# Early keys of pass 2 in larger loads, values' products ahead of scores, and w_in and w_out blocks in pairs, in a two-layer decode kernel on one core

## The chip, the core and the metric

The kernel runs on one core of a Trainium2 chip. Its engines are TensorE (PE, with its weight loads as PEld), VectorE (DVE), ScalarE (ACT), GpSimd (POOL) and SyncE (SP), which here only issues DMAs. Each engine works through its own instructions in the order in which they were written and stops where a semaphore tells it to wait. The metric is the device time of one execution, in microseconds. The kernel before takes 1320.69 us (median of 3 runs, 1320.47 to 1320.93).

## What is computed

Two transformer layers of a decode step, and both layers use the same weights and the same cache. Batch is 2, the model's width 448; there are 16 heads of width 256, a cache of 4096 keys and values for each head and sequence, and a gated feed-forward part of width 1792. All data are float32.

```python
def _A_ref(x, k_cache, v_cache, wq, wo):
    q = (x @ wq).reshape(B, Sq, H, Dh).transpose(0, 2, 1, 3)
    scores = jnp.einsum("bhqd,bhkd->bhqk", q, k_cache) * (Dh ** -0.5)
    p = _softmax(scores, axis=-1)
    o = jnp.einsum("bhqk,bhkd->bhqd", p, v_cache)
    return o.transpose(0, 2, 1, 3).reshape(B, Sq, H * Dh) @ wo

def _B_ref(x, W_gate, W_up, W_down):
    gate = jnp.einsum("bsd,df->bsf", x, W_gate)
    up = jnp.einsum("bsd,df->bsf", x, W_up)
    gate = gate * (gate > 0)
    return jnp.einsum("bsf,fd->bsd", gate * up, W_down)

x = A_x
x = x + _A_ref(_layernorm(x), A_k_cache, A_v_cache, A_wq, A_wo)
x = x + _B_ref(_layernorm(x), B_W_gate, B_W_up, B_W_down)
x = x + _A_ref(_layernorm(x), A_k_cache, A_v_cache, A_wq, A_wo)
x = x + _B_ref(_layernorm(x), B_W_gate, B_W_up, B_W_down)
```

The cache is far larger than the core's memory and is read twice, once for each layer, apart from a few blocks that stay in place between the layers.

## The kernel before, in words

**Pairs and units.** A pair `u` is one head of one sequence; there are 32, numbered 0 to 31 in each pass (a pass is one layer). The keys of a pair are a block of 128 partitions x 8192 numbers, and so are its values. A block has four pieces, `c` = 0 to 3, of 128x2048 numbers, 1 MiB each. One tile, `arena`, holds everything that is read from memory: 27 units of one piece each. Weights come into the same units: `w_head` for each head (query and output weights), and for the feed-forward part seven blocks of `w_in` and four of `w_out`, each 128x1792 or less.

**Loads.** `pending` is a list of loads in a fixed order. `pump` (L116 to L138) takes the first one, asks `units` for as many neighbouring free units as it needs, and writes its DMA on SP's queue (L131). A load of 1 piece is `128x2048`, one of 4 pieces `128x8192`, one of 8 pieces (the keys of a pair together with the values of the pair before it) `128x16384`. A load of 4 or 8 pieces needs 4 or 8 units that stand side by side. `release` frees a unit behind the last instruction that reads it and calls `pump` again. All this is decided when the program is written; on the chip SP waits at each DMA for the readers of the units that it overwrites. So a load waits for its own units and for every load ahead of it in the list.

**Scores and values.** For a pair in the middle, DVE multiplies the whole key block with the query (L378, one instruction of 128x8192) and sums (L386); for some pairs, 5 to 8 of pass 2 among them, 8 of the 32 sums are left to ACT (L382). In the first pairs of pass 2 the pieces are taken one by one: DVE multiplies half a piece in one instruction (L409), ACT sums that half (L411), and DVE multiplies and sums the other half in four instructions (L418). `softmax_max` is L427 on DVE and L429 on POOL, `softmax_exp` L434 and L437 on ACT and L443 on POOL. `weigh` (L462) multiplies the probabilities with the values on PE: 16 matmuls for a pair, four for each piece. Its result stands in `po`, in one half for even and the other for odd pairs. `out_copy` (L475, ACT) and `out_add` (L478, DVE) take it out, `out_turn` (L488, PE), `out_keep` (L501, DVE) and `project` (L511, PE) bring it to the output, and `query` (L338 and L342 on PE, L350 on ACT, L354 on POOL) makes the next head's queries. An instruction of a matmul shows as two records in the profile, so 16 matmuls of L462 are x32.

**The order around the change.** The loop at L527 writes one step for each `u`: scores of `u`, values of `u - 1`, output of `u - 2`. In the first five steps of pass 2 (`mixed`, `u` below `HASTE` = 5) the four pieces of `weigh(u - 1)` are spread between the four pieces of scores; in later steps they come at the end. Pass 2 begins with 20 units kept from pass 1 and its pairs run in another order (`second`). `WHOLE_SECOND` tells which pairs of pass 2 have their keys in loads of 8 pieces; `early` and `at_end` cut others into smaller loads.

Of the kernel before, what the change touches and what calls it, by code (L numbers as in the profile page):

```python
# [14 lines left out]
B, D, H, S, DH, F = 2, 448, 16, 4096, 256, 1792  # L15
P = 128
# [4 lines left out]
UNIT = CT * DH  # L21
NC = NT // CT
BLOCKS, SINGLES = 3, 3
PAIR = 2 * NC
WHOLE_FIRST = range(1, 28)
WHOLE_SECOND = range(9, 29)
KEPT = 20
ALONE = 25

# [41 lines left out]
def two_layers(  # L71
# [20 lines left out]
    arena = consts.tile([P, (BLOCKS * PAIR + SINGLES) * UNIT], F32, name="arena")  # L92
# [4 lines left out]
    units = Arena()  # L97
    pending = []
    at_of = {}
    blocks = set()  # L100

    def source(key, n):
        kind, name, c = key
        if kind in "kv":
            h, b = name
            at = (h * B + b + (kind == "v")) % (H * B)
            c += NC * (kind == "k" and n < PAIR)
            return vk[at, :, c * UNIT : (c + n) * UNIT]
        if kind == "h":
            return w_head[name]  # L110
        if kind == "in":
            return w_in[c]
        return w_out[:, 14 * P * c : min(14 * P * (c + 1), 14 * D)]

    def pump():
        while pending:  # L116
            (kind, name, c), n = pending[0]
            last = at_of.get((kind, name, c - 1)) if kind in "kv" else None
            at = units.take(n, kind, last)
            if at is None:  # L120
                return
            pending.pop(0)
            src = source((kind, name, c), n)
            dst = arena[:, at * UNIT : at * UNIT + src.shape[1]]
            parts = [0, src.shape[1]]
            if not pending:
                parts[1:1] = [src.shape[1] - CLOSE * TAIL]
            elif len(pending) == 1:
                parts[1:1] = [8 * P]
            for i, j in zip(parts, parts[1:]):  # L130
                nc.sync.dma_start(dst[:, i:j], src[:, i:j])  # L131
            for k in range(n):
                key = (kind, name, c + k)
                if n == PAIR:
                    key = ("k", name, k - NC) if k >= NC else ("v", behind[name], k)
                at_of[key] = at + k
            if n >= NC:
                blocks.add((kind, name))  # L138

    def get(*key):  # L140
        at = at_of[key]
        return arena[:, at * UNIT : (at + 1) * UNIT]

    def release(*key):
        units.free.add(at_of.pop(key))
        pump()

    first = [(h, b) for h in range(H) for b in range(B)]
# [3 lines left out]
    def loads(order, whole, cuts):  # L152


        found = [(("h", order[0][0], 0), 1)]

        def some(kind, u):
            c = 0
            for n in cuts.get((kind, u), (NC,)):
                found.append(((kind, order[u], c), n))  # L160
                c += n

        for u, unit in enumerate(order):
# [11 lines left out]
    ffn_loads = [("in", "", c) for c in range(7)] + [("out", "", c) for c in range(4)]  # L175
    n_u = len(first)
    each = (1,) * NC
    twos = (2,) * (NC // 2)
    final = (2, 1, 1)
    at_end = {("k", n_u - 1): twos, ("v", n_u - 2): twos, ("v", n_u - 1): final}  # L180
    of_first = loads(first, WHOLE_FIRST, at_end)
    at_end[("k", n_u - 2)] = twos
    early = {(kind, u): each for u in range(HASTE + 1) for kind in ("kv" if u < HASTE else "k")}
    of_second = loads(second, WHOLE_SECOND, early | at_end)

    keep = {of_second[0][0], *[key for key, _ in of_second if key[0] != "h"][:KEPT]}
    keep.add(("v", second[2], NC - 1))
    of_second = [(key, n) for key, n in of_second if key not in keep]

    heads = [(key, n) for key, n in of_second if key[0] == "h"][:2]  # L190
    of_second = [part for part in of_second if part not in heads]
    of_second[NC - 1 : NC - 1] = heads
    pending += of_first + [(key, 1) for key in ffn_loads]
    pending += of_second + [(key, 1) for key in ffn_loads]

    row = consts.tile([P, 2 * DH], F32, name="row")
    down = consts.tile([P, D], F32, name="down")
# [94 lines left out]
    def inverse():  # L292
        nc.vector.reciprocal(rstd, rstd)

    def attention(order, after, q_first=None, begun=None):
# [6 lines left out]
        n_u = len(order)  # L302
# [67 lines left out]
        def score_block(u, c):  # L370
# [6 lines left out]
            if c == 0:  # L377
                nc.vector.tensor_mul(kt, kt, q_of[u][:, None, :].to_broadcast([P, NT, DH]))  # L378
            shared = 0 if (WHOLE_SECOND if ahead else WHOLE_FIRST)[0] <= u < ALONE else CT
            if c == 0:  # L380
# [10 lines left out]
        def score(u, c):  # L391
# [30 lines left out]
            if not kept:  # L422
                release("k", order[u], c)
# [96 lines left out]
        def if_pair(step, u, *more):  # L520
            if 0 <= u < n_u:
                step(u, *more)
# [4 lines left out]
        for u in range(n_u + 2):  # L527

            mixed = ahead and u < HASTE
            if_pair(score, u, 0)  # L530
            if_pair(out_add, u - 2)
            if_pair(out_turn, u - 2)
            if mixed:
                if_pair(weigh, u - 1, 0)
            if_pair(score, u, 1)
            if mixed:
                if_pair(weigh, u - 1, 1)
            if_pair(score, u, 2)
# [246 lines left out]
def _arrays(np, A_x, A_k_cache, A_v_cache, A_wq, A_wo, B_W_gate, B_W_up, B_W_down, **_):  # L785

    def pairs(cache):
        return cache.transpose(1, 0, 2, 3).reshape(H * B, P, NT * DH)

    rows = FULL * P  # L790
    wq = A_wq.reshape(D, H, DH)
    head = [wq[c * P : (c + 1) * P].transpose(1, 0, 2) for c in range(FULL)]
    head.append(wq[rows:].reshape(TAIL, H, 2, P).transpose(1, 2, 0, 3).reshape(H, P, P))
    wo = A_wo.reshape(H, 2, P, D)
    head += [wo[:, 0], wo[:, 1]]
    full = [w[c * P : (c + 1) * P] for w in (B_W_gate, B_W_up) for c in range(FULL)]
# [4 lines left out]
    found = {  # L801
        "x": A_x,
        "vk": np.concatenate([np.roll(pairs(A_v_cache), 1, 0), pairs(A_k_cache)], axis=2),
        "w_head": np.concatenate(head, axis=2),
        "w_in": np.stack(full),
        "w_out": np.concatenate(
            [c[:, at : at + P] for at in range(0, D, P) for c in chunks], axis=1
        ),
    }
    return {n: np.ascontiguousarray(a) for n, a in found.items()}  # L810


def build(nc, shapes):
    import concourse.tile as _tile

    args = [
        nc.dram_tensor(f"in_{n}_dram", s, F32, kind="ExternalInput").ap() for n, s in shapes.items()
    ]
    for i, (shape, _) in enumerate(_OUTS):
        args.append(nc.dram_tensor(f"out_{i}_dram", shape, F32, kind="ExternalOutput").ap())  # L820
    with _tile.TileContext(nc) as tc:
        two_layers(tc, *args)
# [12 lines left out]
```

## Time and profile before

| | |
|---|---|
| runs of the kernel before | 1320.47, 1320.69, 1320.93 us |
| the profiled execution | 1320.27 us |
| its span, first to last instruction | 1318.5 us |
| read from memory | 562.56 MB, 427 GB/s over the span |
| busy: DVE / PE / POOL / ACT | 1081.6 / 553.7 / 269.0 / 195.6 us |
| DMA queue of SP | 22612 packets, 99.5% of 16 engines' span |

In a row of the timeline the first number is the start in us from the beginning of the span, the second the time it took; then come engine, line, operation, what is written and read, the shape, and in brackets how long the engine had been idle and what ended that. In a row of stages (`A:B`) each engine's busy time is followed by PE's granted clock as a share of full speed, the share of the time in which the 16 DMA engines were busy, and the rate in GB/s. Pass 2 begins near 690 us.

### The profile page before, as it was taken

The page shows a single profiled execution, that of the slowest core. Times are in us where ns is not written, and L with a number is a line of the kernel's source. Part 1 is how long each engine was busy: PE and PEld are TensorE (multiplying, and loading weights), DVE is VectorE, ACT ScalarE, POOL GpSimd, SP SyncE. Part 2 cuts the span into 40 slices and gives each one's busy share as a digit, 9 for nine tenths or more (in the row PEclk, how much of TensorE's full clock was granted, in tenths as well). Part 3 has the DMA queues.
Part 4 walks back from the last instruction along what each step waited for, and adds up shares of the span by engine and source line. Part 5 has one row for each costly group of instructions (what it writes and reads, how often), then busy time and mean ns, then how long its engine had stood idle before and what let it go on. Part 6 is the DMA issues. An engine that isn't in the chain of part 4 may idle for free.

```text
span 1318.5 us, 9085 instructions
## 1 busy us (share of the span) xinstructions
PE 553.7 (42%) x3276; PEld 190.6 (14%) x3276; DVE 1081.6 (82%) x780; ACT 195.6 (15%) x776; POOL 269.0 (20%) x192
## 2 busy tenths in 40 slices
PE   2243342433434324345585444242433424434348
PEld 2011010110111101112141111110111101101113
DVE  4989888898888988888729987798888988877892
ACT  2100000000000000212026513000000000012241
POOL 0002003322133220321001153030123331230210
PEclk9675666656667667666697777666767667666679
DMA  9999999999999999999999999999999999999998
GB/s 408 435 430 429 432 428 437 432 436 434 417 445 435 430 430 426 445 418 430 421 405 416 431 430 435 438 432 430 432 431 436 433 428 436 429 432 425 427 425 334
DMA packets 22665, 563.16 MB, mean 427 GB/s; under 512 B 2520, under 2 KB 2652, under 8 KB 9564
## 3 DMA queue, kind: packets, MB, share of 16 engines
q1 hardware_dynamic: 22612, 562.57, 99.5%
q8 instruction: 26, 0.43, 0.1%
q14 instruction: 19, 0.16, 0.0%
q10 hardware_dynamic: 8, 0.00, 0.0%
HBM read 562.56 MB, written 0.00 MB: 427 GB/s over the span
## 4 chain that ended last, share of the span: by engine, by line
DMA 55%; DVE 32%; PE 7%; POOL 2%; issue 2%; ACT 1%; DVEq 0%; SPq 0%; POOLq 0%; ACTq 0%
DMA arena<-in_vk_dram 54%; DVE arena L378 12%; DVE scores L386 11%; DVE arena L409 3%; DVE down L418 2%; PE po L462 2%; POOL top L429 2%; DVE arena L418 2%; DMA arena<-in_w_out_dram 1%; DVE row L478 1%; PE small L488 1%; PE acc L511 1%; DVE scores L415 1%; ACT arena L411 1%; PE pf L576 1%
## 5 line engine op out<-in xcount | busy, mean ns | idle before, releaser
L378 DVE TENSOR_TENSOR arena<-arena 128x8192 f32<-128x8192 f32 x51 | 443.3, 8692 | 111.0 <-DMA arena<-in_vk_dram 110.9
L386 DVE TENSOR_REDUCE scores<-arena 128x32 f32<-128x8192 f32 (+1 forms) x53 | 431.8, 8148 | 0.0
L488 PE MATMUL small<-ones,row 128*128 128x1 f32 x256 | 62.0, 346 | 686.3 <-DVE row L478 686.3
L462 PE MATMUL po<-arena,probs 128*2 128x512 f32 x2048 | 303.1, 734 | 10.3 <-DMA arena<-in_vk_dram 6.6
L429 POOL PARTITION_ALL_REDUCE top<-mx x64 | 64.6, 1009 | 645.8 <-DVE mx L427 645.8
L443 POOL PARTITION_ALL_REDUCE total<-rs x64 | 176.1, 2752 | 61.3 <-ACT probs L437 60.3
L488 PEld LDWEIGHTS small<-ones,row 128*128 128x128 f32 x256 | 56.5, 308 | 748.9 <-DVE row L478 748.9
L434 ACT ACTIVATE nm<-top,nsr 128x1 f32<-128x1 f32 x64 | 18.8, 294 | 612.4 <-POOL top L429 612.4
L354 POOL PARTITION_BROADCAST arena<-arena x58 | 27.6, 545 | 300.6 <-ACT arena L350 300.6
L462 PEld LDWEIGHTS po<-arena,probs 128*2 128x2 f32 x2048 | 54.8, 96 | 198.3 <-issue 191.2
L338 PE MATMUL pq<-arena,xs 128*33 128x256 f32 x174 | 70.6, 571 | 14.1 <-DMA arena<-in_w_head_dram 14.1
L511 PE MATMUL acc<-arena,oT 128*2 128x448 f32 x128 | 50.9, 894 | 32.1 <-DVE oT L501 32.1
L350 ACT ACTIVATE arena<-pq 33x256 f32<-33x256 f32 x29 | 10.9, 377 | 321.7 <-PE pq L342 321.7
L382 ACT ACTIVATE arena<-arena 128x256 f32<-128x256 f32 x104 | 41.7, 402 | 86.2 <-DVE arena L378 86.2
L478 DVE SCALAR_TENSOR_TENSOR row<-po,lead,row 128x256 f32<-128x256 f32 x64 | 30.7, 479 | 25.8 <-ACT row L475 25.4
L411 ACT ACTIVATE arena<-arena 128x256 f32<-128x256 f32 x117 | 47.1, 404 | 20.4 <-DVE arena L409 20.1
L409 DVE TENSOR_TENSOR arena<-arena 128x1024 f32<-128x1024 f32 (+1 forms) x24 | 42.0, 1748 | 0.0
L338 PEld LDWEIGHTS pq<-arena,xs 128*33 128x33 f32 x174 | 25.3, 162 | 81.3 <-issue 66.7
L475 ACT ACTIVATE row<-po,lead 128x256 f32<-128x256 f32 x64 | 29.1, 455 | 21.2 <-PE po L462 21.2
L418 DVE SCALAR_TENSOR_TENSOR down<-arena,pq 128x256 f32<-128x256 f32 x64 | 26.9, 420 | 5.4 <-DMA arena<-in_vk_dram 3.4
L501 DVE TENSOR_TENSOR oT<-small,ri 128x4 f32<-128x4 f32 x32 | 5.1, 161 | 29.0 <-PE small L488 29.0
L437 ACT ACTIVATE probs<-scores,nm,sr 128x32 f32<-128x32 f32 x64 | 26.4, 413 | 2.1
(145 smaller groups left out, 359.0 us busy)
## 6 DMA issues: line engine op xcount, KB each, us to landing
arena<-in_vk_dram SPq DMA_DIRECT2D x16, 4096.0 KB, 40.0
arena<-in_w_head_dram SPq DMA_DIRECT2D x31, 896.0 KB, 30.9
arena<-in_vk_dram SPq DMA_DIRECT2D x27, 1024.0 KB, 14.9
arena<-in_vk_dram SPq DMA_DIRECT2D x12, 2048.0 KB, 38.5
arena<-in_w_in_dram SPq DMA_DIRECT2D x14, 896.0 KB, 26.2
arena<-in_w_out_dram SPq DMA_DIRECT2D x5, 896.0 KB, 8.9
arena<-in_vk_dram SPq DMA_DIRECT2D x47, 43.4
arena<-in_w_out_dram SPq DMA_DIRECT2D x1, 512.0 KB, 17.3
```

The source lines that it names most:

```text
L338: nc.tensor.matmul(q, xs[:, c, :], w[:, c * DH : (c + 1) * DH], start=(c == 0), stop=False)
L378: nc.vector.tensor_mul(kt, kt, q_of[u][:, None, :].to_broadcast([P, NT, DH]))
L386: nc.vector.reduce_sum(s_of[u][:, shared:], kt[:, shared:, :], axis=AX.X)
L409: nc.vector.tensor_mul(some, some, q_of[u][:, None, :].to_broadcast([P, whole, DH]))
L411: nc.scalar.activation(kt[:, t, :], kt[:, t, :], AF.Copy, accum_out=found[:, t : t + 1])
L418: nc.vector.scalar_tensor_tensor(junk if kept else kt[:, t, :], kt[:, t, :], 1.0, q_of[u], op0=ALU.mult, op1=ALU.mult, accum_out=found[:, ...
L429: nc.gpsimd.partition_all_reduce(mx_of[u], mx, P, RED.max)
L443: nc.gpsimd.partition_all_reduce(total[:, b : b + 1], rs, P, RED.add)
L462: nc.tensor.matmul(po_of[u][32 * t : 32 * t + 2, :], p_of[u][:, n : n + 2], vt[:, 2 * t * DH : (2 * t + 2) * DH], start=(c == 0), stop=(c ...
L478: nc.vector.scalar_tensor_tensor(row[:, :DH], po_of.pop(u)[:, DH:], lead[:, 1:2], row[:, :DH], op0=ALU.mult, op1=ALU.add,)
L488: nc.tensor.matmul(pT_of[u - u % 2][:, c, b : b + 1], row[:, c * P : (c + 1) * P], ones, start=True, stop=True,)
L511: nc.tensor.matmul(acc[at : at + B], oT_of[h][:, c, :], wo[:, c * D : (c + 1) * D], start=(n < 3), stop=(n >= n_u - 3),)
```

## The change

Five edits.

1. In pass 2 the keys of pairs 4 and 5 come as one load of 128x8192 each instead of four of 128x2048. Pair 4 is still scored piece by piece; pair 5 now takes the path of whole blocks (L378, L386).
2. In the first five steps of pass 2 all four pieces of `weigh(u - 1)` are written at the head of the step, ahead of `score(u, 0)`, `out_add(u - 2)` and `out_turn(u - 2)`.
3. Pair 29 of pass 2 has its keys in one load with the values of pair 28, and the keys of pair 30 come as one load instead of two.
4. In the last feed-forward part `w_in` comes as three loads of two blocks and one of one, and the first two blocks of `w_out` as one load. The memory layout of `w_in` becomes 128 rows of all blocks side by side. A unit of such a load is freed when all blocks of the load are done with.
5. `get` and `release` keep account of blocks that lie side by side at another distance than a unit.

```diff
-WHOLE_SECOND = range(9, 29)
+WHOLE_SECOND = range(9, 30)
...
-            return w_in[c]
-        return w_out[:, 14 * P * c : min(14 * P * (c + 1), 14 * D)]
+            return w_in[:, c * F : (c + n) * F]
+        return w_out[:, 14 * P * c : min(14 * P * (c + n), 14 * D)]
...
     def release(*key):
-        units.free.add(at_of.pop(key))
+        held[key] = at_of.pop(key)
+        if key[0] in ("in", "out"):
+            whole = [k for k in together.get(key, (key,))]
+            if any(k in at_of for k in whole):
+                return
+        else:
+            whole = [key]
+        units.free |= {held.pop(k) for k in whole}
         pump()
...
+    last_loads = [(("in", "", c), 2) for c in range(0, 6, 2)]
+    last_loads += [(("in", "", 6), 1), (("out", "", 0), 2), (("out", "", 2), 1), (("out", "", 3), 1)]
...
-    at_end[("k", n_u - 2)] = twos
     early = {(kind, u): each for u in range(HASTE + 1) for kind in ("kv" if u < HASTE else "k")}
+    early |= {("k", u): (NC,) for u in (4, 5)}
...
-    pending += of_first + [(key, 1) for key in ffn_loads]
-    pending += of_second + [(key, 1) for key in ffn_loads]
+    pending += of_first + ffn_loads + of_second + last_loads
...
             mixed = ahead and u < HASTE
+            if mixed:
+                for c in range(NC):
+                    if_pair(weigh, u - 1, c)
             if_pair(score, u, 0)
             if_pair(out_add, u - 2)
             if_pair(out_turn, u - 2)
-            if mixed:
-                if_pair(weigh, u - 1, 0)
             if_pair(score, u, 1)
-            if mixed:
-                if_pair(weigh, u - 1, 1)
             if_pair(score, u, 2)
...
-            if mixed:
-                if_pair(weigh, u - 1, 2)
             if_pair(score, u, 3)
             if_pair(softmax_max, u)
             if_pair(softmax_exp, u)
-            for c in range(NC):
-                if not mixed or c == NC - 1:
+            if not mixed:
+                for c in range(NC):
                     if_pair(weigh, u - 1, c)
```

On PE, at the beginning of pass 2, the rows run from the values of pair 0 (the first `po<-arena,probs`) to the query of the next head. Before:

```order
L462 MATMUL po<-arena,probs 2x512 x16
L488 MATMUL small<-ones,row 128x1 x2
L462 MATMUL po<-arena,probs 2x512 x16
L488 MATMUL small<-ones,row 128x1 x2
L462 MATMUL po<-arena,probs 2x512 x8
L511 MATMUL acc<-arena,oT 2x448 x2
L338 MATMUL pq<-arena,xs 33x256 x3
L342 MATMUL pq<-arena,xs 33x128 x2
L462 MATMUL po<-arena,probs 2x512 x8
```

The same stretch after (L476 is the line of `weigh` there, L502 of `out_turn`, L525 of `project`, L352 and L356 of `query`):

```order
L476 MATMUL po<-arena,probs 2x512 x32
L502 MATMUL small<-ones,row 128x1 x2
L476 MATMUL po<-arena,probs 2x512 x16
L502 MATMUL small<-ones,row 128x1 x2
L525 MATMUL acc<-arena,oT 2x448 x2
L352 MATMUL pq<-arena,xs 33x256 x3
L356 MATMUL pq<-arena,xs 33x128 x2
```

All 16 matmuls of `weigh(u - 1)` now stand ahead of the `out_turn` of the pair before, which stood ahead of them; and none of them stands behind the query any more.

On DVE, in the step `u` = 2 of pass 2, the rows run from the maximum of pair 1's scores to the second piece of pair 2, with the semaphores that each row waits for. Before:

```order
L427 TENSOR_REDUCE mx<-scores 128x1 [waits DVE_49,Activation_49]
L409 TENSOR_TENSOR arena<-arena 128x1024 [waits DMAHW0_49,Pool_49]
L418 SCALAR_TENSOR_TENSOR arena,scores<-arena 128x256 x4
L478 SCALAR_TENSOR_TENSOR row<-po,lead,row 128x256 [waits Activation_49]
L409 TENSOR_TENSOR arena<-arena 128x1024
```

The same stretch after:

```order
L441 TENSOR_REDUCE mx<-scores 128x1 [waits DVE_49,Activation_49]
L423 TENSOR_TENSOR arena<-arena 128x1024 [waits DMAHW0_49,Pool_49]
L432 SCALAR_TENSOR_TENSOR arena,scores<-arena 128x256 x4
L492 SCALAR_TENSOR_TENSOR row<-po,lead,row 128x256 [waits PE_49,Activation_49]
L423 TENSOR_TENSOR arena<-arena 128x1024
```

The instructions stand in the same order, but `out_add` (L478, now L492) has one more wait, on PE. The count that it waits for is the one that PE reaches with the 16th matmul of `weigh(u - 1)`. The same holds in the steps `u` = 3 and `u` = 4, and in no other: elsewhere `out_add(u - 2)` is written ahead of `weigh(u - 1)`.

On SP, the loads at the beginning of pass 2. Before:

```order
L131 DMA arena<-in_w_head_dram 128x1792 x2
L131 DMA arena<-in_vk_dram 128x2048 x20
L131 DMA arena<-in_w_head_dram 128x1792
L131 DMA arena<-in_vk_dram 128x8192 x4
L131 DMA arena<-in_w_head_dram 128x1792
L131 DMA arena<-in_vk_dram 128x8192 x2
L131 DMA arena<-in_vk_dram 128x16384
```

After:

```order
L134 DMA arena<-in_w_head_dram 128x1792 x2
L134 DMA arena<-in_vk_dram 128x2048 x4
L134 DMA arena<-in_vk_dram 128x8192
L134 DMA arena<-in_vk_dram 128x2048 x4
L134 DMA arena<-in_vk_dram 128x8192
L134 DMA arena<-in_vk_dram 128x2048 x4
L134 DMA arena<-in_w_head_dram 128x1792
L134 DMA arena<-in_vk_dram 128x8192 x4
L134 DMA arena<-in_w_head_dram 128x1792
L134 DMA arena<-in_vk_dram 128x8192 x2
L134 DMA arena<-in_vk_dram 128x16384
```

The bytes are the same; eight loads of 1 MiB became two of 4 MiB, and each of these waits until four neighbouring units are free (the first one for the 16th matmul of `weigh(0)`). The first `128x16384` waits, in both kernels, for the sums of pair 7's scores (L386).

More of the change, by code (lines that the diff above doesn't have):

```diff
@@ L99, in two_layers @@
     at_of = {}
+    shift = {}
+    held = {}
+    together = {}
     blocks = set()
@@ L136, in pump @@
                 at_of[key] = at + k
+                if kind in ("in", "out"):
+                    shift[key] = k * (F - UNIT)
+                    together[key] = [(kind, name, c + i) for i in range(n)]
             if n >= NC:
@@ L140, in get @@
     def get(*key):
-        at = at_of[key]
-        return arena[:, at * UNIT : (at + 1) * UNIT]
+        at = at_of[key] * UNIT + shift.get(key, 0)
+        return arena[:, at : at + UNIT]
     def release(*key):
-        units.free.add(at_of.pop(key))
+        held[key] = at_of.pop(key)
[6 more added lines that the diff above has]
+        units.free |= {held.pop(k) for k in whole}
         pump()
@@ L173, in loads @@
         return found
-    ffn_loads = [("in", "", c) for c in range(7)] + [("out", "", c) for c in range(4)]
+    ffn_loads = [(("in", "", c), 1) for c in range(7)] + [(("out", "", c), 1) for c in range(4)]
+    last_loads = [(("in", "", c), 2) for c in range(0, 6, 2)]
+    last_loads += [(("in", "", 6), 1), (("out", "", 0), 2), (("out", "", 2), 1), (("out", "", 3), 1)]
     n_u = len(first)
@@ L804, in _arrays @@
         "w_head": np.concatenate(head, axis=2),
-        "w_in": np.stack(full),
+        "w_in": np.concatenate(full, axis=1),
         "w_out": np.concatenate(
```

## The prediction

> **What bounds the kernel now.** I read the page first, from the slices down to the queues.
>
> ```profile
> DMA  9999999999999999999999999999999999999998
> q1 hardware_dynamic: 22612, 562.57, 99.5%
> ```
>
> The 16 DMA engines are busy in every slice and SP's queue has packets for 99.5% of the span. The program ends when its bytes have passed. It can become faster by costing the DMA engines less for a byte, and slower by letting them run dry. The waits and the stages say how far the compute engines are from that.
>
> ```profile
> DVE arena L378 <- DMA arena<-in_vk_dram: 110.9, 47, 13.1
> 696.00:742.00 46.00, 26.63 (x152) 7.64 (x154) 42.45 (x157) 30.04 (x138) 7.66 (x12) 0.75 1.01 417
> 880.00:1160.00 280.00, 106.43 (x602) 34.55 (x602) 244.49 (x70) 18.86 (x63) 60.52 (x43) 0.67 1.00 432
> ```
>
> DVE waits for data 47 times in the middle of the passes, so it is ahead of memory there. From 696 to 742 us, where pass 2 begins, the DMA engines are full too (1.01), but with 1 MiB loads they move 417 GB/s, with 8 MiB loads 432. DVE is busy for 42.45 of 46 us there: this is the stage where it has least to give away.
>
> How much it has to give away is read at the first 8 MiB load of pass 2, which cannot be issued before pair 7's scores are summed (L386). The rows are SP's issues (the third of them is this load), the landing of the load issued just before it, near 767 us, that sum on DVE, and the shortest landing of any load.
>
> ```profile
> 766.03 35.31 SPq L131 DMA_DIRECT2D arena<-in_vk_dram  x3
> arena<-in_vk_dram SPq DMA_DIRECT2D x1, 4096.0 KB, 44.1
> 794.33 6.54 DVE L386 TENSOR_REDUCE scores<-arena 128x24 f32<-128x6144 f32 x1
> DMA to landing us min/median/max: 4.7/31.9/54.3
> ```
>
> The sum ends at 800.87, the issue follows at 801.0, and the load ahead lands at 811.0. From issue to the first bytes and from the last bytes to the landing some time passes; the shortest load (4.7 us from issue to landing, of which one of 0.9 MB takes 2.1 us at 432 GB/s) bounds both together by 2.6 us. I take 2.2. The **reserve** is 811.0 - 801.0 - 2.2 = 7.8 us: if DVE comes to the end of pair 7's scores more than 7.8 us later than now, the DMA engines stand still for the rest.
>
> **The change part by part.**
>
> *Fewer loads.* 1 MiB takes 2.515 us at 417 GB/s and 2.427 at 432, 0.088 more; an 8 MiB load has an eighth of its own overhead in that, so a load costs about 0.10 us beside its bytes. Pairs 4 and 5 save six loads, pair 29 one, pair 30 one, `w_in` three, `w_out` one: 12 x 0.10 = 1.2 us, 0.6 of it after the first 8 MiB load. Its ends: 0 and, if the whole stretches at 417 and (at the end) 420 GB/s went at 432, 46 x 15/432 + 48 x 12/432 = 2.9 us.
>
> ```profile
> 1262.00:1310.00 48.00, 32.90 (x223) 11.27 (x223) 27.24 (x38) 17.22 (x70) 3.43 (x4) 0.83 1.01 420
> ```
>
> [...]
>
> *Values ahead of scores.* This is the part that decides. The steps 2, 3 and 4 of pass 2 get a new wait: `out_add(u - 2)` on DVE (L478) waits for the last matmul of `weigh(u - 1)`, which now stands ahead of it. Behind it in DVE's queue are three pieces of scores, the maximum, and everything that follows. In step 2 the profile now shows
>
> ```profile
> 710.17 0.19 DVE L427 TENSOR_REDUCE mx<-scores 128x1 f32<-128x32 f32 x1 [0.41 <-ACT arena L411]
> 712.38 0.19 ACT L437 ACTIVATION_READ_ACCUMULATOR probs<-scores,nm,sr 128x1 f32 x1
> 712.96 0.48 DVE L478 SCALAR_TENSOR_TENSOR row<-po,lead,row 128x256 f32<-128x256 f32 x1
> 713.50 1.01 PE L488 MATMUL small<-ones,row 128*128 128x1 f32 x4 [6.96 <-DVE row L478]
> 714.45 5.80 PE L462 MATMUL po<-arena,probs 128*2 128x512 f32 x32
> ```
>
> Pair 1's probabilities are ready at 712.57, DVE reaches `out_add` at 712.96 without waiting, and `weigh(1)` goes on beside the scores. After the change `weigh(1)` starts at about 712.6 and DVE stands from 712.96 until it is done. How long are 16 matmuls?
>
> ```profile
> 701.23 5.31 PE L462 MATMUL po<-arena,probs 128*2 128x512 f32 x32 [3.65 <-ACT probs L437]
> 725.73 3.57 PE L462 MATMUL po<-arena,probs 128*2 128x512 f32 x16
> 732.59 1.90 PE L462 MATMUL po<-arena,probs 128*2 128x512 f32 x16
> 738.65 5.31 PE L462 MATMUL po<-arena,probs 128*2 128x512 f32 x32
> ```
>
> Eight cost 3.57 us at the low granted clock and 1.90 at the full one, so 16 lie between 3.8 and 7.1; the three whole ones of this stage took 5.31, 5.80 and 5.31. PE will have idled before each, so I take 5.5. DVE gets there 0.4 after the start; with 0.1 for the semaphore it stands for 5.2 us, three times: **15.6 us**. Ends: 3 x 3.5 and 3 x 6.8.
>
> [...]
>
> *The query in step 3* now follows an idle PE. It took 2.77 us before (729.89 to 732.66); one after an idle stretch took 5.2.
>
> ```profile
> 729.89 0.92 PE L511 MATMUL acc<-arena,oT 128*2 128x448 f32 x4 [0.59 <-DVE oT L501]
> 734.70 0.18 DVE L427 TENSOR_REDUCE mx<-scores 128x1 f32<-128x32 f32 x1 [2.35 <-ACT arena L411]
> 757.96 1.66 PE L511 MATMUL acc<-arena,oT 128*2 128x448 f32 x4 [6.49 <-DVE oT L501]
> 762.12 1.06 PE L342 MATMUL pq<-arena,xs 128*33 128x128 f32 x4
> ```
>
> ACT's sums stand behind the query's copy, and DVE's maximum already waited 2.35 us for them, so a longer query adds to DVE: between 0 and 2.4 us. I take 1.8, since the clock mostly falls over 4 us without work.
>
> *Pair 5 as a block.* Its step took 18.76 us from maximum to maximum (746.06 to 764.82); the odd pair 7, which is a block already, takes 18.61 (782.37 to 800.98). I take 0; the POOL step that stands 8.8 us beside L378 then delays pair 4's probabilities, but DVE does not wait for them longer than in these steps.
>
> ```profile
> 746.06 0.19 DVE L427 TENSOR_REDUCE mx<-scores 128x1 f32<-128x32 f32 x1 [0.40 <-ACT arena L411]
> 764.82 0.19 DVE L427 TENSOR_REDUCE mx<-scores 128x1 f32<-128x32 f32 x1 [3.19 <-ACT arena L411]
> 782.37 0.19 DVE L427 TENSOR_REDUCE mx<-scores 128x1 f32<-128x32 f32 x1
> 800.98 0.19 DVE L427 TENSOR_REDUCE mx<-scores 128x1 f32<-128x32 f32 x1
> 765.18 8.82 POOL L429 PARTITION_ALL_REDUCE top<-mx  x1 [0.54 <-DVE mx L427]
> ```
>
> *Waiting for four units at once.* Pair 4's load waits for the end of `weigh(0)`, 706.54, and its bytes come some 1.5 us later, near 708. The queue holds bytes until about 706.7 (the load ahead of it lands at 707.6), so about 1 us runs dry here. It comes off the later hole, whose end DVE sets, and adds nothing.
>
> *The end.* After the last feed-forward load PE works block by block.
>
> ```profile
> 1310.86 1.07 PE L669 MATMUL po<-arena,row 128*32 128x128 f32 x28
> 1312.10 0.96 PE L669 MATMUL pf<-arena,row 128*32 128x128 f32 x26 [0.17 <-DMA arena<-in_w_out_dram]
> 1314.98 0.47 PE L669 MATMUL pf<-arena,row 128*32 128x64 f32 x18 [0.17 <-DMA arena<-in_w_out_dram]
> ```
>
> The first two blocks of `w_out` now arrive together, when the second does. PE starts three blocks of 1.07 to 1.15 us at 1312.10 instead of 1310.86 and gets to the last one at 1315.4 instead of 1314.98: +0.4 (0 to 0.8).
>
> *Sum.* DVE late by 15.6 + 1.8 = 17.4; less the reserve 7.8, 9.6 us of standing DMA engines; less 0.6, plus 0.4: +9.4. Against the profiled execution's 1320.27 (1.8 over its span, 0.4 under the median) that is 1329.7; against the median 1330.1. The hand-overs from PE to DVE and ACT are in it with 0.1 us for each batch only, while the waits on ACT above last 0.41 and 0.40; I add an estimated 0.1 for each of the three batches and say **1330.5**.
>
> **The rivals.**
>
> *The wait bites little, and fewer loads win.* If PE were done when DVE comes, in each step within 2.6 us of it, the lateness stays under the reserve, and the sum is -1.2 + 0.4: 1319.9. For it speaks that DVE does wait for memory from 817 us on and catches up there; against it that 16 matmuls take 3.8 us even at full clock and start only 0.4 us before DVE arrives. From 2.6 us a step on it ends on the slower side.
>
> *PE stays warm.* 3.8 us for each batch, 3.5 of standing, no longer query: 10.5 - 7.8 - 0.2 = +2.5, 1323.2. Against it: PE idles 5 us ahead of each batch.
>
> *PE stays cold.* 6.8 + 6.8 + 6.8 + 2.4 = 22.8, less 7.8 and 0.2: +14.8, 1335.5.
>
> *Larger loads are worth the upper end*, and nothing runs dry: -2.9 + 0.4, 1318.2. [...]
>
> **How the numbers follow.** The sum above has a chance of 0.78 with a range of its own of 1326 to 1334; no bite 0.09, warm 0.05, cold 0.06, larger loads 0.02. The range 1325 to 1335.5 leaves out the fast cases and half the cold one, under 2 in 10. 0.2% is 2.6 us, about what a measurement of this kernel can tell from no change: slower by more holds the sum, cold and half of warm, 0.87; within it half of warm and the no-bite case, 0.11; faster by more 0.02.
>
> **What would show it.** Right: three idles of some 5 us on DVE before `out_add`, ended by PE, between 712 and 755 us; its maxima of pairs 4 to 7 some 17 us late; a slice near 811 us where the DMA engines stand for 8 to 11 us; the first 8 MiB load issued near 818. Wrong: `out_add` waiting less than 2.6 us, or DMA share near 1 all through, or a reserve that was larger because other loads fill the hole.

## The result, and the profile after

The changed kernel takes 1335.42 us (median of 5 runs, 1334.29 to 1335.81) against 1320.69 (1320.47 to 1321.08) for the kernel before: 14.7 us slower, a ratio of 1.011 with a 95% interval of 1.0096 to 1.0125. The forecast was 1330.5 us, in a range of 1325 to 1335.5. The direction and the mechanism were right; 4.9 of the 14.7 us, a third, had not been foreseen. That the time lies inside the range is luck: it is 0.1 us below the upper end, two of the five runs lie above it, and the sum's own range, 1326 to 1334, missed it. The profiled execution has a span of 1333.6 us, 15.1 more than before.

The slices and the queue of the changed kernel, in the page:

```profile
DMA  9999999999999999999999996999999999999997
q1 hardware_dynamic: 20884, 562.57, 98.3%
```

One slice, the 25th (800 to 833 us), now has a 6. Two stretches in it and shortly before it, first of the kernel after, then of the kernel before (start and end, length, busy time of the engines, granted clock, DMA share, GB/s):

```profile
706.00:707.50 1.50, 0.41 (x4) 0.00 (x0) 1.50 (x9) 1.50 (x7) 0.00 (x0) 1.00 0.38 109
811.60:821.20 9.60, 8.41 (x50) 3.04 (x50) 8.00 (x5) 3.93 (x19) 1.87 (x4) 0.72 0.00 0
```

```profile
706.00:707.50 1.50, 0.54 (x8) 0.00 (x0) 1.50 (x9) 1.50 (x8) 0.00 (x0) 1.00 0.98 404
811.60:821.20 9.60, 4.95 (x32) 0.73 (x24) 5.58 (x2) 2.97 (x14) 0.73 (x2) 0.85 1.00 432
```

From 706 to 707.5 us the DMA engines are busy for 0.38 of the time only, and from 811.6 to 821.2 us they move nothing at all. Summed over the packets of the trace the two holes are 2.3 and 11.1 us long.

What stands in front of the second hole is read in the timeline of the kernel after: PE's products, `out_add` on DVE (L492), some maxima (L441; those of pairs 2, 3, 4 and 7), and SP's issues, of which the third in the row is the first 8 MiB load.

```profile
713.03 6.09 PE L476 MATMUL po<-arena,probs 128*2 128x512 f32 x32 [6.62 <-ACT row L489]
730.57 5.85 PE L476 MATMUL po<-arena,probs 128*2 128x512 f32 x32 [10.15 <-ACT row L489]
751.41 5.67 PE L476 MATMUL po<-arena,probs 128*2 128x512 f32 x32 [4.94 <-ACT row L489]
```

```profile
719.27 0.48 DVE L492 SCALAR_TENSOR_TENSOR row<-po,lead,row 128x256 f32<-128x256 f32 x1 [6.35 <-PE po L476]
727.76 0.19 DVE L441 TENSOR_REDUCE mx<-scores 128x1 f32<-128x32 f32 x1 [0.40 <-ACT arena L425]
736.57 0.48 DVE L492 SCALAR_TENSOR_TENSOR row<-po,lead,row 128x256 f32<-128x256 f32 x1 [6.12 <-PE po L476]
748.52 0.19 DVE L441 TENSOR_REDUCE mx<-scores 128x1 f32<-128x32 f32 x1 [3.84 <-ACT arena L425]
757.24 0.48 DVE L492 SCALAR_TENSOR_TENSOR row<-po,lead,row 128x256 f32<-128x256 f32 x1 [5.94 <-PE po L476]
765.73 0.19 DVE L441 TENSOR_REDUCE mx<-scores 128x1 f32<-128x32 f32 x1 [0.39 <-ACT arena L425]
820.31 0.19 DVE L441 TENSOR_REDUCE mx<-scores 128x1 f32<-128x32 f32 x1
784.26 36.35 SPq L134 DMA_DIRECT2D arena<-in_vk_dram  x3
```

DVE stands three times, 18.4 us in all, and each time PE ends the wait. Its maximum of pair 7 comes at 820.31 instead of 800.98, 19.3 us late, and the load goes out at 820.28 (784.26 + 36.35, less 0.33 for the issue itself) instead of 801.01. That is the forecast mechanism, at the forecast place.

The rest is at the end. The last rows of the waits and of the chain tell it: DVE's maxima of pairs 28 and 29, the first product of pair 29's keys between them, and the maxima of pairs 30 and 31, of the kernel after and of the kernel before.

```profile
1248.85 0.19 DVE L441 TENSOR_REDUCE mx<-scores 128x1 f32<-128x32 f32 x1
1252.39 8.69 DVE L392 TENSOR_TENSOR arena<-arena 128x8192 f32<-128x8192 f32 x1 [3.36 <-DMA arena<-in_vk_dram]
1269.31 0.19 DVE L441 TENSOR_REDUCE mx<-scores 128x1 f32<-128x32 f32 x1
1286.71 0.19 DVE L441 TENSOR_REDUCE mx<-scores 128x1 f32<-128x32 f32 x1
1302.00 0.19 DVE L441 TENSOR_REDUCE mx<-scores 128x1 f32<-128x32 f32 x1 [0.52 <-ACT arena L425]
```

```profile
1236.69 0.18 DVE L427 TENSOR_REDUCE mx<-scores 128x1 f32<-128x32 f32 x1
1236.79 8.68 DVE L378 TENSOR_TENSOR arena<-arena 128x8192 f32<-128x8192 f32 x1
1255.26 0.18 DVE L427 TENSOR_REDUCE mx<-scores 128x1 f32<-128x32 f32 x1
1270.58 0.19 DVE L427 TENSOR_REDUCE mx<-scores 128x1 f32<-128x32 f32 x1 [0.52 <-ACT arena L411]
1285.86 0.19 DVE L427 TENSOR_REDUCE mx<-scores 128x1 f32<-128x32 f32 x1 [0.52 <-ACT arena L411]
```

At pair 28 DVE is 12.2 us late, at pair 31 16.1. Pair 29 takes 20.5 us instead of 18.6: its keys now land with the values of pair 28 as one load, and DVE waits 3.36 us for the landing, at 1252.37 us, where it had gone on at once. Pair 30 takes 17.4 instead of 15.3: as one load it is scored as a whole block, of whose 32 sums ACT takes 8 instead of 16. In both kernels everything behind pair 31's maximum hangs on it, but in the chain of before a landing stands between:

```profile
1300.25 14.69 DMA arena<-in_w_out_dram
```

The chain of the kernel after has no such row near its end. Its last landing is this one, the load of pairs 28 and 29, and from there on it is DVE, PE, ACT and POOL alone:

```profile
1207.99 44.38 DMA arena<-in_vk_dram
```

So the changed kernel ends by computing, no longer by memory, and of the 16.1 us by which DVE is late the span shows 15.1. The first product with `w_out` comes 25.0 us after pair 31's maximum in both kernels, at 1310.86 us before and here after:

```profile
1326.98 0.96 PE L680 MATMUL po<-arena,row 128*32 128x128 f32 x26
```

From there to the end it takes 6.6 us instead of 7.6: about 1 us went into the waits for `w_out` that the kernel before had.

### The profile page after: what moved, and what is told of

Read it like the earlier page. It is cut to its first block, busy times and chain, and to the rows that moved or that the text cites. A ratio compares the mean times of both kernels' runs of the same rounds, so it can differ in the third digit from the quotient of the medians.

```text
span 1333.6 us, 9012 instructions
## 1 busy us (share of the span) xinstructions
PE 572.0 (43%) x3276; PEld 193.2 (14%) x3276; DVE 1083.4 (81%) x768; ACT 190.4 (14%) x752; POOL 291.4 (22%) x192
## 4 chain that ended last, share of the span: by engine, by line
DMA 54%; DVE 27%; PE 11%; POOL 4%; issue 2%; ACT 1%; DVEq 0%; SPq 0%; POOLq 0%; ACTq 0%
DMA arena<-in_vk_dram 54%; DVE arena L392 11%; DVE scores L400 10%; POOL top L443 4%; PE po L476 4%; DVE arena L432 2%; DVE arena L423 1%; PE small L502 1%; PE pf L587 1%; PE acc L525 1%; PE pq L352 1%; DVE row L492 1%; DVE down L432 1%; ACT arena L425 1%; PE po L680 0%
## 5 line engine op out<-in xcount | busy, mean ns | idle before, releaser
L392 DVE TENSOR_TENSOR arena<-arena 128x8192 f32<-128x8192 f32 x53 | 460.7, 8692 | 104.9 <-DMA arena<-in_vk_dram 104.9
L400 DVE TENSOR_REDUCE scores<-arena 128x32 f32<-128x8192 f32 (+1 forms) x55 | 444.9, 8089 | 0.0
L502 PE MATMUL small<-ones,row 128*128 128x1 f32 x256 | 60.4, 340 | 663.1 <-DVE row L492 663.1
L476 PE MATMUL po<-arena,probs 128*2 128x512 f32 x2048 | 310.5, 750 | 30.9 <-ACT row L489 21.7
L443 POOL PARTITION_ALL_REDUCE top<-mx x64 | 77.3, 1208 | 633.2 <-DVE mx L441 633.2
L457 POOL PARTITION_ALL_REDUCE total<-rs x64 | 185.7, 2902 | 61.3 <-ACT probs L451 61.3
L502 PEld LDWEIGHTS small<-ones,row 128*128 128x128 f32 x256 | 55.0, 300 | 722.1 <-DVE row L492 722.1
L476 PEld LDWEIGHTS po<-arena,probs 128*2 128x2 f32 x2048 | 54.5, 97 | 234.2 <-issue 202.9
L352 PE MATMUL pq<-arena,xs 128*33 128x256 f32 x174 | 77.9, 618 | 14.5 <-DMA arena<-in_w_head_dram 14.5
L492 DVE SCALAR_TENSOR_TENSOR row<-po,lead,row 128x256 f32<-128x256 f32 x64 | 30.7, 479 | 46.7 <-ACT row L489 28.3
L525 PE MATMUL acc<-arena,oT 128*2 128x448 f32 x128 | 51.7, 906 | 30.9 <-DVE oT L515 30.9
L396 ACT ACTIVATE arena<-arena 128x256 f32<-128x256 f32 x120 | 48.0, 402 | 87.3 <-DVE arena L392 87.3
L425 ACT ACTIVATE arena<-arena 128x256 f32<-128x256 f32 x89 | 35.8, 404 | 29.8 <-DVE arena L423 29.8
L352 PEld LDWEIGHTS pq<-arena,xs 128*33 128x33 f32 x174 | 26.0, 166 | 83.1 <-issue 67.8
L489 ACT ACTIVATE row<-po,lead 128x256 f32<-128x256 f32 x64 | 29.2, 456 | 22.7 <-PE po L476 22.7
L356 PE MATMUL pq<-arena,xs 128*33 128x128 f32 x116 | 25.9, 367 | 0.0
```

The costliest lines, as they stand in the source:

```text
L352: nc.tensor.matmul(q, xs[:, c, :], w[:, c * DH : (c + 1) * DH], start=(c == 0), stop=False)
L396: nc.scalar.activation(kt[:, t, :], kt[:, t, :], AF.Copy, accum_out=s_of[u][:, t : t + 1])
L400: nc.vector.reduce_sum(s_of[u][:, shared:], kt[:, shared:, :], axis=AX.X)
L425: nc.scalar.activation(kt[:, t, :], kt[:, t, :], AF.Copy, accum_out=found[:, t : t + 1])
L443: nc.gpsimd.partition_all_reduce(mx_of[u], mx, P, RED.max)
L457: nc.gpsimd.partition_all_reduce(total[:, b : b + 1], rs, P, RED.add)
```

## The experiments

**The order alone, the loads alone, and the key loads at the end.** Theory A was read from the trace of the kernel after: the order costs by DVE's lateness less a reserve, and the key loads of pairs 29 and 30 cost besides. Theory B was the prediction: everything belongs to the order.

The kernel before with the order of the change:

```diff
             mixed = ahead and u < HASTE
+            if mixed:
+                for c in range(NC):
+                    if_pair(weigh, u - 1, c)
             if_pair(score, u, 0)
...
-                if_pair(weigh, u - 1, 0)
...
```

> The kernel before with only the values' products moved ahead in the five mixed steps. Theory A: DVE stands three times for about 6 us and is 19.3 us late at pair 7; 6.7 of it were free, so +12.6: 1333.3 us, a hole of about 12.6 us near 810 and none near 706, and the end as before (DVE from pair 28's maximum to pair 31's in 49.2 us). Rival B (all of the 14.7 us belong to the order): 1335.4 us.

Measured: 1333.31 us, a ratio of 1.0093 (1.0076 to 1.011). DVE stood 6.28, 6.08 and 5.93 us, and the DMA engines 12.5 us near 815 us. The kernel before took 1320.54 us beside it, so the order accounts for 12.8 of the 14.7 us (10.0 to 14.5 by the interval).

The kernel before with edit 3's loads at the end:

```diff
-WHOLE_SECOND = range(9, 29)
+WHOLE_SECOND = range(9, 30)
...
-    at_end[("k", n_u - 2)] = twos
```

> The kernel before with only pair 29's keys in one load with pair 28's values and pair 30's keys as one load. Theory A: from pair 28's maximum to pair 31's DVE takes 53.2 us instead of 49.2, of which about 1.0 is absorbed by waits for w_out and 0.2 saved by two loads: 1323.5 us. Rival B (the prediction): two loads fewer and nothing else, 1320.5 us.

Measured: 1324.48 us, 1.0029 (1.0018 to 1.0039). The row of pair 29's first product there:

```profile
1240.58 8.69 DVE L377 TENSOR_TENSOR arena<-arena 128x8192 f32<-128x8192 f32 x1 [3.38 <-DMA arena<-in_vk_dram]
```

Two loads fewer made the kernel 3.9 us slower (2.4 to 5.1 by the interval). In this trace, too, DVE takes 53.2 us from pair 28's maximum to pair 31's. Pairs 29 and 30 were not run apart; of the 4.0 us the trace of the kernel after puts 1.9 on pair 29 and 2.1 on pair 30. The opposite, the changed kernel without edit 3:

```diff
-WHOLE_SECOND = range(9, 30)
+WHOLE_SECOND = range(9, 29)
...
+    at_end[("k", n_u - 2)] = twos
```

> The changed kernel with the key loads of pairs 29 and 30 as before. Theory A: 1335.4 - 4.0 + 1.0 + 0.2 = 1332.6 us; PE waits for w_out at the end again. Rival B: 1335.6 us.

Measured: 1333.42 us, 1.0099 (1.0084 to 1.0114), 2.0 us less than the changed kernel. This difference is less sure than the 3.9 us: the two intervals overlap, and in the two traces, 2.1 us apart, DVE is 1.0 us less late already at pair 28 (11.2 us instead of 12.2), whose keys edit 3 leaves as they were. From there to pair 31's maximum DVE takes 49.2 us instead of 53.2. So edit 3 does cost 4.0 us of DVE's time here too, but most of it comes back, among other things because without edit 3 PE waits for the pair of `w_out` blocks:

```profile
1323.27 1.26 PE L681 MATMUL po<-arena,row 128*32 128x128 f32 x26 [1.06 <-DMA arena<-in_w_out_dram]
```

With the order's 12.8 the 2.0 makes 14.8, the whole of the 14.7 us, though each of the two terms is known to some 2 us only.

**The changed loads in the old order** missed both expectations.

```diff
             mixed = ahead and u < HASTE
-            if mixed:
-                for c in range(NC):
-                    if_pair(weigh, u - 1, c)
             if_pair(score, u, 0)
...
+            if mixed:
+                if_pair(weigh, u - 1, 0)
...
```

> The changed kernel with the values' products back in the order of before, loads as changed. Theory A (the trace of after): the order costs 12.6 us by the time the first 8 MiB load goes out, and on top of it the key loads at the end (pairs 29 and 30) make DVE 4.0 us longer from pair 28's maximum to pair 31's; before had about 1.0 us of waits for w_out that absorb a part. Without the order's stall the hole of 2.3 us near 706 is no longer hidden behind DVE. So 1320.7 + 2.3 - 0.7 + 4.0 - 1.0 = 1325.3 us, no DVE idle ended by PE before out_add, no hole near 811. Rival B (the prediction): the end costs 0.4, loads save 1.2, the hole near 706 is 1 us or adds nothing: 1319.9 to 1320.9 us.

Measured: 1329.1 us, 1.0065 (1.005 to 1.008). There was no hole near 811 us, but the one near 706 was 5.9 us long instead of 2.3, and these 3.6 us are nearly the whole miss against theory A. What SP waited for from 695 to 712 us (line waited for, us in total, times, longest), in this run and then in the kernel after:

```profile
SPq L134 <- DVE arena L432: 14.0, 3, 9.9
```

```profile
SPq L134 <- PE po L476: 6.5, 1, 6.5
```

In the kernel after pair 4's block waits for the values of pair 0, which are freed by `weigh(0)`. In the old order the four pieces of `weigh(0)` are written between the pieces of pair 1's scores, so that pair 1's keys are complete ahead of pair 0's values. The row says that the block waits for DVE there, which sums pair 1's last piece until 710.3 us; the block goes out at 710.8. That it is put into the place of pair 1's keys is concluded from this. Edit 2 is what lets the block of edit 1 go out earlier, at 706.5 us; the two can't be priced apart.

**What the wait is for.** If the order costs only through DVE's wait, it should cost nothing where DVE has no such wait. Two ways of that: `out_add` written ahead of the products, and the two halves of `po` as two tiles.

```diff
+            if_pair(score, u, 0)
+            if_pair(out_add, u - 2)
             if mixed:
                 for c in range(NC):
                     if_pair(weigh, u - 1, c)
-            if_pair(score, u, 0)
-            if_pair(out_add, u - 2)
             if_pair(out_turn, u - 2)
```

> The changed kernel with the values' products written behind out_add instead of ahead of it (score piece 0, out_add, the 16 matmuls, out_turn, pieces 1 to 3), so that PE still has them ahead of out_turn and the query, but DVE has nothing to wait for. Theory A (the order costs only through DVE's wait on PE): no idle ended by PE before out_add, DVE at most 2 us late at pair 7, no hole near 811; what stays is the hole of 2.3 us near 706 and the 4.0 us of pairs 29 and 30, less 0.4 for loads and 1.0 of waits for w_out that these absorb: 1325.6 us. Rival B (the move costs by itself: the query late in step 3, the batches on a cold PE): DVE over 6.7 us late at pair 7 and over 1330 us.

```diff
-    po_all = ps_o.tile([P, 2, 2 * DH], F32, name="po")
+    po_all = [ps_o.tile([P, 2 * DH], F32, name=n) for n in ("po", "po_odd")]
...
-                po_of[u] = po_all[:, u % 2]
+                po_of[u] = po_all[u % 2]
```

> The changed kernel, in its own order, with the two halves of po as two tiles. Even and odd pairs write different halves, so out_add needs nothing of the products that stand ahead of it; if the wait comes only from the two halves being one tile, it goes. Theory A: out_add no longer waits for PE, nor the products for out_copy; 1325.6 us as in the run with out_add first. Rival B (the wait is one of the data): DVE stands three times for 6 us, 1335 us.

Measured: 1326.94 us (1.0047, 1.003 to 1.0064) and 1325.27 us (1.0038, 1.0023 to 1.0053), both at the value of theory A within their spread. In the second the order is exactly that of the change, and PE starts as soon as the probabilities are there:

```profile
714.51 4.90 PE L477 MATMUL po_odd<-arena,probs 128*2 128x512 f32 x32 [6.09 <-ACT probs L452]
725.79 6.08 PE L477 MATMUL po<-arena,probs 128*2 128x512 f32 x32 [5.84 <-ACT probs L452]
740.01 5.80 PE L477 MATMUL po_odd<-arena,probs 128*2 128x512 f32 x32 [4.58 <-ACT probs L452]
```

The batches take about as long as in the kernel after (5.6 us in the mean instead of 5.9), but DVE does not stand for them: its rows of `out_add` in these steps show no wait. The wait was one of names, not of data. Even and odd pairs write different halves, and the half that `out_add` reads had long been finished; since both halves were one tile, the wait was for the last instruction that had written any of it. For the same reason the products in the changed kernel waited for `out_copy` on ACT (L489 in the rows above) and not for the probabilities.

The last test of this is the order with two tiles on the loads of before:

> The kernel before with the values' products ahead in all five mixed steps and the two halves of po as two tiles; loads as before. Theory A (the order costs only through the wait on the shared tile): DVE under 3 us late at pair 7, no hole near 706 or 811, 1320.7 us within 0.2%. Rival B (the order also changes which units come free first, and the first 8 MiB load then waits for products on PE, as in the run with the order moved up to step 2): up to 2.5 us more, 1323.2 us, and the load's issue ended by PE.

Measured: 1321.22 us, 1.0004 (0.9995 to 1.0013), which is no change. The order by itself is free.

**How much of DVE's lateness is free.** The order moved up to step 2, and up to step 3:

```diff
             mixed = ahead and u < HASTE
+            moved = mixed and u <= 2
+            if moved:
+                for c in range(NC):
+                    if_pair(weigh, u - 1, c)
             if_pair(score, u, 0)
...
-            if mixed:
+            if mixed and not moved:
                 if_pair(weigh, u - 1, 0)
...
```

> The kernel before with the values' products ahead only up to step 2, so that DVE stands once for PE. Theory A (reserve of 6.7 us): DVE 6.3 us late at pair 7, no hole near 811 beyond 0.5 us, 1320.7 us (up to 1321.2). Rival B (lateness passes on in full): 1327.0 us.

> The same up to step 3, so that DVE stands twice and the query of step 3 comes late. Theory A: DVE 13.8 us late at pair 7, less 6.7: a hole of 7.1 us near 811, 1327.8 us. Rival B (lateness passes on in full): 1334.5 us; Rival C (the prediction's reserve of 7.8): 1326.7 us.

Measured: 1323.1 us (1.0017, 1.0007 to 1.0026) and 1330.53 us (1.0075, 1.006 to 1.009), 2.4 and 2.7 us above theory A. Here DVE was not the last one. Of SP's waits from 760 to 830 us in the run up to step 2, the longest is ended by PE: the load had been given units that hold values, and it went out only when their products were done, 2.3 us behind pair 7's maximum. In the run up to step 3 it was 2.7.

```profile
SPq L131 <- PE po L462: 19.8, 2, 18.5
```

Counted by the issue itself it comes out straight. The first 8 MiB load is the third issue of these rows, of the runs up to step 2, up to step 3, and in all five steps:

```profile
769.66 38.79 SPq L131 DMA_DIRECT2D arena<-in_vk_dram  x3
```

```profile
780.18 39.03 SPq L131 DMA_DIRECT2D arena<-in_vk_dram  x3
```

```profile
784.73 36.39 SPq L131 DMA_DIRECT2D arena<-in_vk_dram  x3
```

It went out at 808.12, 818.88 and 820.79 us, that is 7.1, 17.9 and 19.8 later than in the kernel before, and the spans were 1319.6, 1330.2 and 1332.0 us, 1.1, 11.7 and 13.5 longer. The difference is 6.0, 6.2 and 6.3. So about 6.2 us of lateness are free in these three traces, and every further microsecond is paid in full. The count is one of the traced executions: that of the run up to step 2 was its fastest of ten, 1321.45 us.

**The hole near 706 us by itself.** Two tiles, and the key loads of pairs 29 and 30 as before, leave of the change only what has not been priced yet (both diffs stand above).

> The changed kernel with two tiles for po and the key loads of pairs 29 and 30 as before, so that of the change only pair 4's and 5's blocks, the order without its wait, and the pairs of w_in and w_out are left. It measures the hole near 706 by itself. Theory A (each microsecond that the DMA engines stand there is lost, since nothing later covers it): 2.3 to 3.4 us of hole, less 0.8 for ten loads fewer, plus 0.4 for the pairs of blocks: 1322.6 to 1323.7 us. Rival B (the hole is made up for later): 1320.3 us.

Measured: 1322.89 us, 1.0012 (1.0003 to 1.0021). The hole was 3.1 us long, and the kernel 2.1 us slower. Where nothing later covers it, it is paid, for the most part (0.4 to 2.8 us by the interval). In the changed kernel it was covered: the first 8 MiB load went out with the end of pair 7's sums, whatever the earlier hole, and the kernel is not slower than the order and edit 3 make it, as far as their sum is known.

**Pairs of `w_in` and `w_out`, and a version that was to be faster.**

The first of the two is the kernel before with edit 5 and all of edit 4; the lines that make the pairs:

```diff
+    last_loads = [(("in", "", c), 2) for c in range(0, 6, 2)]
+    last_loads += [(("in", "", 6), 1), (("out", "", 0), 2), (("out", "", 2), 1), (("out", "", 3), 1)]
```

> The kernel before with only the w_in and w_out blocks of the last feed-forward part in pairs, that is four loads fewer. The prediction: -0.4 for loads, +0.4 for the first blocks of w_out that come together: 1320.7 us. Rival (the run of the changed kernel with the key loads of before, in which PE waited 1.06 us for the pair of w_out blocks and the end from pair 31's maximum took 1.9 us longer): 1321.5 to 1322.6 us.

Measured: 1321.18 us, 1.0005 (0.9997 to 1.0014), no change that can be told; up to 1.8 us more lie in the interval, so the lower end of the rival is not excluded. PE waits 0.83 us for the pair:

```profile
1311.90 0.96 PE L683 MATMUL po<-arena,row 128*32 128x128 f32 x26 [0.83 <-DMA arena<-in_w_out_dram]
```

```diff
...
+    early[("k", 5)] = (NC,)
...
-CLOSING = 2
+CLOSING = 3
...
     at_end[("k", n_u - 2)] = twos
+    at_end[("k", n_u - 3)] = twos
```

> A version meant to be faster: the kernel before with pair 5's keys as one load, w_in in pairs, w_out as before, and pair 29's keys as two loads of two pieces with the split of DVE and ACT that pairs 30 and 31 have. Theory A: six loads fewer, 0.6 us, and DVE 3 us earlier at pair 31, so that the DMA engines alone set the end: 1320.0 us. Rival (pair 5's block waits for four neighbouring units as pair 4's did, and a hole opens near 715 us): 1322 us or more.

Measured: 1320.84 us, 0.9999 (0.9991 to 1.0008). Pair 5's block opened no hole, but neither five loads fewer in all nor the other split of pair 29 gave anything: its step took 18.1 us instead of 18.6, since DVE waited 3.36 us for ACT's half. Pair 31's maximum came at 1286.18 us, 0.3 us later than in the kernel before and not 3 us earlier.

```profile
1255.60 0.19 DVE L443 TENSOR_REDUCE mx<-scores 128x1 f32<-128x32 f32 x1 [3.36 <-ACT arena L427]
```

No version that was run beats the kernel before.

## Why the prediction was right, and where not

*The new wait.* Right in place, number and releaser: three idles before `out_add`, in steps 2, 3 and 4, ended by PE. Each was forecast as 5.2 us and took 6.35, 6.12 and 5.94, so that 15.6 became 18.4. Of the 2.8 us between, 1.1 is the length of the batches (5.5 taken, 5.87 in the mean). Most of the rest is their start, 0.4 to 0.5 us later than taken: the step "`weigh(1)` starts at about 712.6" reckoned with the probabilities, while the products waited for `out_copy`, which ACT does behind them. The shared tile that gave DVE its wait gave PE one too. A batch does not take the same time in every run: in the run with the key loads of before, in which nothing of this stage differs, the same three waits were 5.26, 5.57 and 5.19 us, 16.0 in all (the last section says what differs).

*The query in step 3* was taken as 1.8 us; DVE's wait for ACT in that step went from 2.35 to 3.84, 1.5 us. After 4.50 us of idle the output and the query took 4.25 us there (742.22 to 746.47) instead of 2.77. The clock had fallen, as taken (granted 0.50 from 742.2 to 745.3 us); in the trace of the kernel before, the six idles of PE of over 4 us between 690 and 800 us (4.54 to 11.09) all ended at a granted clock of 0.50, the two of 3.65 and 3.63 us at 1.00. *Pair 5 as a block* was taken as 0, and from pair 4's maximum on the lateness fell by 0.3 us. Together DVE was 19.3 us late, not 17.4.

*The reserve* was too large: 7.8 us against 6.2 by three runs. The step that failed is "from issue to the first bytes and from the last bytes to the landing", put at 2.2 us together. In the trace of the kernel before the packets of the 8 MiB load begin at 807.3 to 809.8 us on the 16 engines, 2.5 us ahead of the landing at 811.0 in the middle, and in the trace after 1.0 us passes from the issue to the first packet: 3.5 us together, which leaves 6.5. The 2.6 us from the shortest load, taken as a bound, did not hold; why was not followed up.

*The hole near 706 us* was forecast as about 1 us that "comes off the later hole". It was 2.3, and came off the later hole. The 1.5 us from the issue of pair 4's block to its bytes were an estimate; in the trace after it is issued at 706.5 us and its packets begin at 707.4 to 708.4 on the 16 engines, 1.0 to 1.9 us later. That it is paid where no later hole follows was shown by the runs with two tiles and in the old order, to the accuracy of their intervals.

*The end* is where the prediction was wrong in kind. "Pair 29 one, pair 30 one" stood in it as 0.2 us saved, and the step was costed at +0.4 for `w_out` alone. That a larger load lands later as a whole was reckoned for `w_out` and not for the keys of pairs 29 and 30, although they stand on the path that sets the end: 3.9 us by themselves, some 2.0 on top of the rest. With them the sum closes: 19.3 - 6.2 + 2.0 = 15.1, the difference of the spans; the 2.0 in it has the uncertainty named above. By the trace of the kernel after alone, DVE is 12.2 us late at pair 28, falls 4.0 further behind by pair 31, and 1.0 comes back behind it.

*Fewer loads* were taken as 1.2 us in all, and no run shows them: with four fewer at the end, and with five fewer, the intervals hold no change. They are about 1 us wide to either side, so savings of 0.4 and 0.5 us, which the forecast's 0.10 a load would give, are neither shown nor refuted.

*The rivals.* "PE stays cold" came out nearest in time, at 1335.5, but not by its mechanism: the batches were not at the low clock throughout (a granted clock of 0.59 to 0.63 over the three, 0.50 being the low one). The 5.4 us by which the spans missed the sum were 1.9 of lateness, 1.6 of reserve, 1.6 at the end and 0.6 of loads, less the 0.3 that had been added for the hand-overs. "Bites little" and "stays warm" fell by the length of the idles, and the rival of larger loads by the runs above.

## What to carry to other kernels

Work that is moved ahead of a reader in program order can give that reader a wait, even where the two touch different parts of one tile: here splitting `po` in two took 10 us away from the changed kernel without moving an instruction. The price of lateness is not the lateness but what exceeds the reserve at the next load that hangs on it (13.5 of 19.8 us with the order alone), and the reserve is to be read from the issue and the first packet, not from the landing (here 6.5 us that way and 7.8 the other, where three runs showed 6.2). A load made larger near the end of a program is to be priced by when its landing lets the consumer start (here 3.36 us later for pair 29), and by which path of the code the consumer then takes (here 17.4 us instead of 15.3 for pair 30); the saved overhead of a load did not show in any run here.

## What was not expected of the hardware

The same 16 matmuls of step 2, `weigh(1)`, took 4.90 us in the changed kernel with two tiles, 6.09 in the kernel after and 6.34 in the run with `out_add` first. In the kernel after they had a granted clock of 0.59, in the changed kernel with the key loads of before 0.72. The program up to that place differs in nothing that PE does. The traces show when the clock changed, here in the kernel after and then in the other:

```profile
713.03:718.05 5.02, 5.02 (x24) 0.84 (x28) 0.00 (x0) 1.54 (x8) 0.13 (x1) 0.50 0.95 410
718.05:719.12 1.07, 1.06 (x12) 0.10 (x4) 0.00 (x0) 0.00 (x0) 0.00 (x0) 1.00 1.03 436
```

```profile
713.38:716.22 2.84, 2.84 (x16) 0.54 (x20) 0.00 (x0) 1.54 (x8) 0.12 (x1) 0.50 1.23 531
716.22:718.38 2.16, 2.15 (x20) 0.29 (x12) 0.00 (x0) 0.00 (x0) 0.00 (x0) 1.00 0.63 273
```

Each batch ran at half clock first (granted 0.50) and at full clock (1.00) from one moment on, 5.02 us into it in one trace and 2.84 us in the other. Counting the time at half clock as half, both did 3.58 us of work at full clock (5.02/2 + 1.07 and 2.84/2 + 2.16). In the trace of the kernel before this batch, from 714.45 us, ran at half clock for 4.44 us and at full clock for 1.36, again 3.58. So in these three traces its length is set by the moment of the change alone. The two moments of the rows above lie 1.83 us apart, while the batches begin within 0.35 us of each other: the moment does not follow from where the batch begins. In the trace of the kernel before the changes come at 718.89, 722.30, 729.13 and 739.37 us, that is 3.41, 6.83 and 10.24 us after one another; what sets them was not shown.

A longer batch makes DVE's wait longer here (6.35 us before the first `out_add` in the kernel after, 5.26 in the other), but the spread of the times is not larger for it: the changed kernel's five runs lie within 1.5 us, and the kernel before spread over 0.6 us in five runs and over 2.1 in 27.
